# A decode-attention kernel: key loads moved four sets ahead of value loads, value products moved five sets behind scores

## The chip, the cores and the metric

The kernel runs on one core of a Trainium2 chip. The metric is device time in microseconds (us) of one execution. The core has a matrix engine (TensorE; PE in the profile, its weight loads PEld), VectorE (DVE), ScalarE (ACT), GpSimd (POOL), SyncE (SP, which here only issues transfers) and 16 DMA engines.

## The reference, cut to what matters

One decode step for a batch of 8 sequences. A layer norm of x, then attention over the last 1024 cached positions with 32 query heads and 8 key/value heads, an output projection, and a gate from a small gated feed-forward block:

```python
W = min(4096, max(256, Sk // 4))                      # 1024 of 4096 cached positions
q = (xn @ wq).reshape(B, 1, 32, 128)                  # B = 8
k, v = k_cache[:, :, Sk - W:], v_cache[:, :, Sk - W:] # 8 kv heads, 4 query heads each
p = softmax(q k^T / sqrt(128))
s = (p v).reshape(B, 1, 4096) @ wo                    # wo: 4096 x 512
g = silu((gelu(xn @ w_gate) * (xn @ w_up)) @ w_down)
out = x + s * g
```

The window of keys and that of values are 16 MiB each in bf16; with wq and wo (4 MiB each) and the feed-forward weights (5.25 MiB) 47.46 MB have to be read.

## The kernel before, in words

**Sets.** There are 64 pairs of a kv head and a sequence. Four pairs (one kv head, four sequences) make a *set*: there are NQ = 16 sets, and each has 1 MiB of keys and 1 MiB of values. A set lies in SBUF as 32 chunks of 128 x 128 (8 KB in each partition). I call the loads K0 to K15 and V0 to V15; V14 is the values of set 14. Sets 2h and 2h + 1 are kv head h, and `wo` is loaded in eight blocks of 0.5 MiB, one for each kv head, wo0 to wo7.

**Loads.** All large loads are issued by SP, in program order, at the top of the program (lines 164 to 178): four feed-forward blocks, two blocks of w_down, four of wq, then the first keys, and then in a loop over q: keys of set q + LAG, values of set q, and after every second set a block of wo. With LAG = 2 the order is K0 K1 K2 V0 K3 V1 wo0 K4 V2 ... K15 V13 wo6 V14 V15 wo7. Every load but wo takes the next of NRING = 16 buffers of `ring`, in turn; a load waits until what was in its buffer has been read.

**The main loop** (lines 523 to 546) is written out by hand in the order in which each engine's queue takes it. Step q works on the keys of set q and, LAG steps behind, on the values of set v = q - LAG, so that there are NQ + LAG steps. A step has four quarters, i = 0 to 3, one for each pair of the set:

- `transposes` (L389) of the *next* pair's eight key chunks into PSUM, evicted to `kT` by VectorE (L396) or ScalarE (L398) in turn. In quarter 3 the next pair belongs to set q + 1, so there the step first needs K(q + 1).
- in quarter 0 `sums(v)`: four matmuls (L461) for the softmax's denominators, and on VectorE their reduction and reciprocal;
- `values` (L487): eight matmuls of the pair's value chunks with the probabilities pT. Each moves VC = 4 column groups of 16 where one is needed, and VCW = 8 in the last LAG sets; only the first group of `o_ps` is used. Where the groups would run past the set, one is moved. `o_ps` has one PSUM buffer.
- in quarter 1 `max_all(q - 1)`, a transpose (L426) and three small VectorE operations (L428, L433, L436), and in quarter 2 `exponentials(q - 1)`: a matmul (L447) that adds the shift, and the exponential on ScalarE (L456), which writes pT;
- `scores` (L406) of the current pair: eight matmuls;
- in quarters 2 and 3 of every second step two heads each of `project` (L513), 16 matmuls in a step, for the kv head whose two sets are done.

After the four quarters VectorE does `normalise(v)` (L498), which reads `o_ps` and releases it, and `max_keys(q)` (L417, L421).

When the last values are done, the last four heads are projected (16 matmuls, L513), multiplied by the gate (L552), transposed (L555), added to x (L557) and stored (L558). The results of the matmuls on `idle_ps` (L256) and of the spare column groups are not read.

Of the kernel before, what the change touches and what calls it, by code (L numbers as in the profile page):

```python
# [17 lines left out]
def kernel(  # L18
# [30 lines left out]

    nc = tc.nc
    ctx.enter_context(tc.manual_schedule())

    B, Sq, D = A_x.shape
    Hkv, Sk, Dh = A_k_cache.shape[1], A_k_cache.shape[2], A_k_cache.shape[3]
# [15 lines left out]
    NCS = QG * NSC  # L72
# [6 lines left out]
    NQ = NG // QG  # L79
    QC = QG * rep  # L80
    SH = B // QG
    LAG = 2

    consts = ctx.enter_context(tc.tile_pool(name="consts", bufs=1))
    weights = ctx.enter_context(tc.tile_pool(name="weights", bufs=1))
# [1 line left out]
    ffn_sb = ctx.enter_context(tc.tile_pool(name="ffn_sb", bufs=1))  # L87
    ring = ctx.enter_context(tc.tile_pool(name="ring", bufs=NRING))
    kT_pool = ctx.enter_context(tc.tile_pool(name="kT_pool", bufs=3))
    p_pool = ctx.enter_context(tc.tile_pool(name="p_pool", bufs=4))  # L90
    small = ctx.enter_context(tc.tile_pool(name="small", bufs=2))
    ps_misc = ctx.enter_context(tc.tile_pool(name="ps_misc", bufs=1, space=PSUM))
    ps_kT = ctx.enter_context(tc.tile_pool(name="ps_kT", bufs=2, space=PSUM))
# [15 lines left out]
    NL = NCS * Dh  # L109
    q_sb, up_sb, dn_sb, k_sb, v_sb = {}, {}, {}, {}, {}  # L110

    def buffer(n):
        return ring.tile([P, NL], BF16, name="ring_sb")[:, 0:n]

    def load_set(cache, q):
        hkv, b = divmod(q * QG, B)
        t = buffer(NL)
        nc.sync.dma_start(
            out=t,
            in_=cache[b : b + QG, hkv, win0:Sk, :].rearrange(  # L120
                "g (e c) d -> e g (c d)", c=NCS
            ),
        )
        return t

    def load_k(q):
        k_sb[q] = load_set(A_k_cache, q)

    def load_v(q):
        v_sb[q] = load_set(A_v_cache, q)  # L130

    def load_q(k):
        q_sb[k] = buffer(Hq * Dh)
        nc.sync.dma_start(out=q_sb[k], in_=A_wq.rearrange("(p k) n -> p k n", k=NDC)[:, k, :])  # L134
# [20 lines left out]
    def load_wo(hkv):  # L155
        nc.sync.dma_start(
            out=wo_sb[:, hkv * rep : (hkv + 1) * rep, :],
            in_=A_wo[hkv * rep * Dh : (hkv + 1) * rep * Dh, :].rearrange(
                "(k p) d -> p k d", p=P
            ),  # L160
        )
# [6 lines left out]
        load_down(n)  # L168
    for k in range(NDC):
        load_q(k)  # L170
    for q in range(LAG):
        load_k(q)
    for q in range(NQ):
        if q + LAG < NQ:
            load_k(q + LAG)
        load_v(q)
        if q % SH == SH - 1:
            load_wo(q // SH)
# [57 lines left out]
    for i in range(2):  # L236
        t = consts.tile([MK + QG, QC], BF16, name=f"diag{i}")
# [146 lines left out]
    def transposes(g):  # L384
        q, i = divmod(g, NB)
        kT_ps = ps_kT.tile([P, W], BF16, name="kT_ps")
        for c in range(NSC):
            n = i * NSC + c
            nc.tensor.transpose(  # L389
                kT_ps[:, c * P : (c + 1) * P],  # L390
                k_sb[q][:, n * Dh : (n + 1) * Dh],
                ident,
            )
        kT[g] = kT_pool.tile([P, W], BF16, name="kT")
        if i % 2 == 0:
            nc.vector.tensor_copy(out=kT[g], in_=kT_ps)  # L396
        else:
            nc.scalar.copy(out=kT[g], in_=kT_ps)  # L398
# [80 lines left out]
    def values(g):  # L479
        q, i = divmod(g, NB)  # L480
        if i == 0:
            o_ps[q] = ps_o.tile([P, VCW, QC], FP32, name="o_ps")
        for c in range(NSC):
            n = i * NSC + c
            wide = VC if q < NQ - LAG else VCW
            wide = wide if n + wide <= NCS else 1
            nc.tensor.matmul(  # L487
                o_ps[q][:, 0:wide, :],
                v_sb[q][:, n * Dh : (n + 1) * Dh],
                pT[q][:, n : n + wide, :],  # L490
                start=(n == 0),
                stop=(n == NCS - 1),
                skip_group_check=True,
            )
# [26 lines left out]


    transposes(0)
    for q in range(NQ + LAG):
        v = q - LAG
        for i in range(NB):
            g = q * NB + i
            if g + 1 < NG:
                transposes(g + 1)
            if v >= 0:  # L530
                if i == 0:
                    sums(v)
                values(v * NB + i)
            if i == 1 and 1 <= q <= NQ:
                max_all(q - 1)
            if g < NG:
                scores(g)
            if i == 2 and 1 <= q <= NQ:
                exponentials(q - 1)
            if v >= SH and v % SH == 0 and i >= NB // 2:  # L540
                for h in range(2):
                    project((v // SH - 1) * rep + (i - NB // 2) * 2 + h)
        if v >= 0:
            normalise(v)
        if q < NQ:
            max_keys(q)
# [42 lines left out]
```

## Time and profile before

| what | value |
|---|---|
| median of 3 runs | 128.93 us (128.87 to 129.06) |
| profiled execution | 129.06 us, of which its span is 127.3 us |
| busy, share of the span | PE 81%, PEld 66%, DVE 47%, ACT 35%, POOL 1% |
| loads, share of 16 DMA engines' span | 93.4%, mean 375 GB/s over the span |
| key set load: issue to landing (median) | 19.0 us |
| value set load: issue to landing (median) | 19.0 us |
| granted TensorE clock | 1.000 |

The profile is of one execution; the span goes from the first to the last instruction, and the execution's time is 1.76 us longer than it. Times in the rows count from the span's start. "busy" of PE holds overlapping matmuls, so a matmul's mean duration is not its pitch: eight matmuls with 128 columns start some 54 ns apart while each is listed with 219 ns. An arrow in brackets names what ended the idle time before an instruction.

### The profile page before, as it was taken

How to read it: one execution, taken by the hardware profiler on the slowest of the kernel's cores; microseconds unless marked ns; L12 is line 12 of the kernel's file. 1: busy time of each engine (PE TensorE's matmuls, PEld its weight loads, DVE VectorE, ACT ScalarE, POOL GpSimd, SP SyncE). 2: the span in 40 equal slices, each digit the busy share in tenths (PEclk: the TensorE clock that was granted, in tenths of full speed). 3: DMA queues.
4: the chain of work that ended last, by engine and by line, in shares of the span. 5: the costliest groups of instructions: out<-in, count | busy, mean ns of one | idle time of the engine just before them, and what ended most of it. 6: DMA issues, size and time to landing. Idle time of an engine off the chain costs nothing.

```text
span 127.3 us, 4703 instructions
## 1 busy us (share of the span) xinstructions
PE 103.6 (81%) x2131; PEld 83.6 (66%) x2131; DVE 60.0 (47%) x189; ACT 44.5 (35%) x54; POOL 1.2 (1%) x7
## 2 busy tenths in 40 slices
PE   0999999897889987988788597769967995899880
PEld 0355646655679877877777586658956874797770
DVE  3700030101487666584765546464736674665631
ACT  4000130000646663434365434434343454354100
POOL 3000000000000000000000000000000000000000
PEclk9999999999999999999999999999999999999999
DMA  3999999999999999999999999999999999999500
GB/s 93 408 421 396 351 421 422 420 420 420 417 420 414 394 417 417 400 403 430 409 388 415 420 405 400 415 420 397 409 414 418 397 413 420 398 408 387 188 1 3
DMA packets 11860, 47.76 MB, mean 375 GB/s; under 512 B 816, under 2 KB 6720, under 8 KB 7232
## 3 DMA queue, kind: packets, MB, share of 16 engines
q1 hardware_dynamic: 11824, 47.46, 93.4%
q8 instruction: 16, 0.26, 0.8%
q10 hardware_dynamic: 16, 0.01, 0.1%
q14 instruction: 4, 0.03, 0.1%
HBM read 47.46 MB, written 0.01 MB: 373 GB/s over the span
## 4 chain that ended last, share of the span: by engine, by line
DMA 72%; PE 10%; SPq 9%; DVE 4%; ACT 1%; issue 1%; DVEq 0%
DMA ring_sb<-in_A_v_cache_dram 44%; DMA ring_sb<-in_A_k_cache_dram 28%; SPq L134 5%; PE kT_ps L389 3%; PE o_ps L487 3%; SPq L148 2%; SPq L141 2%; DVE kT L396 2%; PE sc_ps L406 2%; ACT kT L398 1%; PE sc_ps L447 1%; DVE diag L433 1%; DVE nm L428 1%; DVE diag L436 1%; PE sums_ps L461 0%
## 5 line engine op out<-in xcount | busy, mean ns | idle before, releaser
L398 ACT COPY kT<-kT_ps 128x1024 bf16<-128x1024 bf16 x32 | 32.4, 1012 | 53.9 <-PE kT_ps L389 53.9
L389 PE MATMUL kT_ps<-ident,ring_sb 128*128 128x128 bf16 x512 | 38.8, 218 | 6.0 <-DMA ring_sb<-in_A_k_cache_dram 6.0
L396 DVE COPY kT<-kT_ps 128x1024 bf16<-128x1024 bf16 x32 | 22.1, 691 | 33.5 <-PE kT_ps L389 33.5
L389 PEld LDWEIGHTS <-ring_sb 128*128 128x128 bf16 x512 | 29.2, 97 | 10.1 <-DMA ring_sb<-in_A_k_cache_dram 9.5
L487 PE MATMUL o_ps<-pT,ring_sb 128*128 128x64 bf16 (+2 forms) x512 | 25.6, 193 | 6.6 <-DMA ring_sb<-in_A_v_cache_dram 5.1
L487 PEld LDWEIGHTS <-ring_sb 128*128 128x128 bf16 x512 | 21.3, 98 | 9.4 <-DMA ring_sb<-in_A_v_cache_dram 8.4
L406 PE MATMUL sc_ps<-qT_all,kT 128*128 128x16 bf16 x512 | 22.6, 170 | 1.2 <-ACT kT L398 0.5
L406 PEld LDWEIGHTS <-kT 128*128 128x128 bf16 x512 | 18.8, 96 | 2.5 <-ACT kT L398 1.0
L256 PE MATMUL idle_ps<-ones_w 128*128 128x512 bf16 x66 | 19.6, 437 | 0.0
L417 DVE TENSOR_REDUCE mx<-sc_ps 128x16 f32<-128x512 f32 x16 | 10.9, 681 | 0.3 <-PE sc_ps L406 0.3
L456 ACT ACTIVATE pT<-sc_ps 128x512 bf16<-128x512 f32 x16 | 9.6, 598 | 3.0 <-PE sc_ps L447 3.0
L256 PEld LDWEIGHTS <-ones_w 128*128 128x128 bf16 x66 | 6.1, 106 | 6.7 <-issue 3.4
L447 PE MATMUL sc_ps<-diag,spread 68*128 68x512 bf16 x16 | 6.0, 376 | 2.3 <-DVE diag L436 0.4
L513 PEld LDWEIGHTS <-wo_sb 128*128 128x128 bf16 x128 | 4.8, 96 | 3.1 <-issue 2.3
L461 PE MATMUL sums_ps<-pT,ones_pp 128*128 128x128 bf16 x64 | 6.2, 219 | 0.1
L513 PE MATMUL sT_ps<-oT_all,wo_sb 128*128 128x8 bf16 x128 | 5.3, 166 | 0.3 <-DVE oT_all L498 0.3
L370 PEld LDWEIGHTS <-ring_sb 128*128 128x128 bf16 x128 | 3.7, 96 | 2.0 <-DMA ring_sb<-in_A_wq_dram 0.8
L469 DVE TENSOR_REDUCE recip<-sums_ps 128x16 f32<-128x128 f32 x16 | 4.5, 283 | 0.4 <-PE sums_ps L461 0.4
L498 DVE TENSOR_TENSOR oT_all<-o_ps,recip 128x16 bf16<-128x16 f32 x16 | 3.5, 220 | 2.5 <-PE o_ps L487 2.5
L428 DVE TENSOR_REDUCE nm<-mxT_ps 16x1 f32<-16x128 f32 x16 | 4.3, 270 | 0.4 <-PE mxT_ps L426 0.4
L295 PEld LDWEIGHTS <-ring_sb 128*128 128x128 bf16 x112 | 3.6, 101 | 1.3 <-issue 0.8
L461 PEld LDWEIGHTS <-ones_pp 128*128 128x128 bf16 x64 | 4.3, 98 | 0.1
(57 smaller groups left out, 45.4 us busy)
## 6 DMA issues: line engine op xcount, KB each, us to landing
ring_sb<-in_A_k_cache_dram SPq DMA_DIRECT2D x16, 1024.0 KB, 19.0
ring_sb<-in_A_v_cache_dram SPq DMA_DIRECT2D x16, 1024.0 KB, 19.0
ring_sb<-in_A_wq_dram SPq DMA_DIRECT2D x4, 1024.0 KB, 14.8
wo_sb<-in_A_wo_dram SPq DMA_DIRECT2D x8, 512.0 KB, 18.0
ring_sb<-in_B_w_gate_dram SPq DMA_DIRECT2D x2, 896.0 KB, 4.8
ring_sb<-in_B_w_up_dram SPq DMA_DIRECT2D x2, 896.0 KB, 8.2
ring_sb<-in_B_w_down_dram SPq DMA_DIRECT2D x2, 896.0 KB, 13.2
x_sb<-in_A_x_dram ACTq DMA_DIRECT2D x1, 8.0 KB
```

Source lines behind the costliest of these rows:

```text
L134: nc.sync.dma_start(out=q_sb[k], in_=A_wq.rearrange("(p k) n -> p k n", k=NDC)[:, k, :])
L256: nc.tensor.matmul(idle_ps, ones_w[:, 0:P], ones_w, start=True, stop=True)
L389: nc.tensor.transpose(kT_ps[:, c * P : (c + 1) * P], k_sb[q][:, n * Dh : (n + 1) * Dh], ident,)
L396: nc.vector.tensor_copy(out=kT[g], in_=kT_ps)
L398: nc.scalar.copy(out=kT[g], in_=kT_ps)
L406: nc.tensor.matmul(sc[q][:, i * NSC + c, :], kT[g][:, c * P : (c + 1) * P], qT_all[:, b : b + QG, hkv * rep : (hkv + 1) * rep], start=(i = ...
L417: nc.vector.tensor_reduce(out=mx, in_=sc[q].rearrange("p c n -> p n c"), axis=AX.X, op=ALU.max)
L447: nc.tensor.matmul(sc[q], spread, shift[q].unsqueeze(1).to_broadcast([MK + QG, NCS, QC]), start=False, stop=True, skip_group_check=True,)
L456: nc.scalar.activation(out=pT[q], in_=sc[q], func=ACT.Exp, scale=inv_sqrt_dh)
L461: nc.tensor.matmul(sums_ps, ones_pp, pT[q][:, c * SC : (c + 1) * SC, :], start=(c == 0), stop=(c == NCS // SC - 1),)
L487: nc.tensor.matmul(o_ps[q][:, 0:wide, :], v_sb[q][:, n * Dh : (n + 1) * Dh], pT[q][:, n : n + wide, :], start=(n == 0), stop=(n == NCS - 1 ...
L513: nc.tensor.matmul(sT_ps[0][:, d, :], wo_sb[:, h, d * P : (d + 1) * P], oT_all[:, h, :], start=(h == 0 and d == 0), stop=(h == Hq - 1), sk ...
```

## The change

LAG is split in two: LEAD = 4 says how many sets the key loads run ahead of the value loads, and LAG = LEAD + 1 = 5 how many steps the value products run behind the scores. The order of the loads becomes K0 K1 K2 K3 K4 V0 K5 V1 wo0 K6 V2 ... K15 V11 wo5 V12 V13 wo6 V14 V15 wo7, and the loop has 21 steps instead of 18. The values of the last set come in two loads, of 24 and of 8 chunks (6 KB and 2 KB in each partition), each with its own ring buffer. pT gets 7 buffers instead of 4. Chunks are handed out as lists of views, which changes no instruction. Since the line that chooses between VC and VCW compares with NQ - LAG, the eight-group form now holds for sets 11 to 15 instead of 14 and 15.

```diff
-    LAG = 2
+    LEAD = 4
+    LAG = LEAD + 1
+    VH = 3 * NCS // 4
...
-    p_pool = ctx.enter_context(tc.tile_pool(name="p_pool", bufs=4))
+    p_pool = ctx.enter_context(tc.tile_pool(name="p_pool", bufs=7))
...
-    def load_set(cache, q):
+    def load_set(cache, q, c0, c1):
+
         hkv, b = divmod(q * QG, B)
-        t = buffer(NL)
+        t = buffer((c1 - c0) * Dh)
         nc.sync.dma_start(
             out=t,
             in_=cache[b : b + QG, hkv, win0:Sk, :].rearrange(
                 "g (e c) d -> e g (c d)", c=NCS
-            ),
-        )
-        return t
+            )[:, :, c0 * Dh : c1 * Dh],
+        )
+        return [t[:, c * Dh : (c + 1) * Dh] for c in range(c1 - c0)]
 
     def load_k(q):
-        k_sb[q] = load_set(A_k_cache, q)
+        k_sb[q] = load_set(A_k_cache, q, 0, NCS)
 
     def load_v(q):
-        v_sb[q] = load_set(A_v_cache, q)
+        parts = (0, NCS) if q < NQ - 1 else (0, VH, NCS)
+        v_sb[q] = []
+        for c0, c1 in zip(parts, parts[1:]):
+            v_sb[q] += load_set(A_v_cache, q, c0, c1)
...
-    for q in range(LAG):
+    for q in range(LEAD):
         load_k(q)
     for q in range(NQ):
-        if q + LAG < NQ:
-            load_k(q + LAG)
+        if q + LEAD < NQ:
+            load_k(q + LEAD)
         load_v(q)
...
-                k_sb[q][:, n * Dh : (n + 1) * Dh],
+                k_sb[q][n],
...
-                v_sb[q][:, n * Dh : (n + 1) * Dh],
+                v_sb[q][n],
```

## The prediction

> **What bounds the kernel now.** I read the page first (slices, then the chain), then the chain of waits in order of time, then the stages around the end, then the timeline of TensorE (PE). Columns of the slices are fortieths of the span, about 3.18 us each.
>
> ```profile
> PE   0999999897889987988788597769967995899880
> PEclk9999999999999999999999999999999999999999
> DMA  3999999999999999999999999999999999999500
> ```
>
> The 16 DMA engines are busy from the second slice until about 118 us, PE never reaches its limit for long, and its granted clock is full in all slices. So until about 118 us the time is that of 47.46 MB through the queues; the change moves no byte out. What it can alter lies behind the last megabytes. The chain in order of time (start, duration, what):
>
> ```profile
> 79.21 17.96 DMA ring_sb<-in_A_v_cache_dram
> ...
> 99.72 18.05 DMA ring_sb<-in_A_v_cache_dram
> 117.76 0.05 issue
> 117.81 1.07 PE o_ps L487 x16
> ...
> 119.87 0.39 PE sc_ps L447
> ...
> 120.29 0.61 ACT pT L456
> ...
> 120.93 0.38 PE sums_ps L461 x4
> 121.32 1.57 PE o_ps L487 x32
> 122.89 0.02 issue
> 122.91 0.24 DVE oT_all L498
> 123.15 0.04 issue
> 123.19 0.56 PE sT_ps L513 x16
> ```
>
> V14 lands at 117.76. But from there the chain isn't a transfer: it is the softmax of the last key set (maximum, shift L447, exponential L456, sums L461), and only then 32 value matmuls of set 15. The stages show that V15 isn't awaited (columns: window, length, busy PE, PEld, DVE, ACT, POOL, PEclk, DMA share, GB/s):
>
> ```profile
> 118.50:119.00 0.50, 0.50 (x12) 0.49 (x10) 0.27 (x2) 0.00 (x0) 0.00 (x0) 1.00 0.60 244
> 120.50:121.00 0.50, 0.43 (x18) 0.36 (x14) 0.23 (x1) 0.38 (x1) 0.00 (x0) 1.00 0.22 70
> 121.00:121.50 0.50, 0.50 (x11) 0.50 (x11) 0.14 (x1) 0.00 (x0) 0.00 (x0) 1.00 0.02 6
> ```
>
> Everything, the last wo block behind V15 included, is in at about 121.05, and V15 about 0.5 MiB before that, near 120; its matmuls start at 121.15. The project matmuls of the last head start at 123.19; the rest of the span (4.1 us) is the output's path, which the change doesn't touch. So I count in "start of the last projection": 123.19 now.
>
> Before 117 us PE waits for both kinds of load in each step:
>
> ```profile
> 106.13 0.62 PE L389 MATMUL kT_ps<-ident,ring_sb 128*128 128x128 bf16 x8 [0.94 <-DMA ring_sb<-in_A_k_cache_dram]
> 108.63 0.41 PE L487 MATMUL o_ps<-pT,ring_sb 128*128 128x64 bf16 x8 [0.78 <-DMA ring_sb<-in_A_v_cache_dram]
> 112.72 0.61 PE L389 MATMUL kT_ps<-ident,ring_sb 128*128 128x128 bf16 x8
> 117.31 0.38 PE L461 MATMUL sums_ps<-pT,ones_pp 128*128 128x128 bf16 x4
> ```
>
> **Where the keys and values land after the change.** From V10 (79.21 + 17.96 = 97.17) to V14 (117.76) before's order moves K13, V11, wo5, K14, V12, K15, V13, wo6, V14: 7 x 1 MiB + 2 x 0.5 = 8 MiB in 20.59 us, 2.57 us per MiB. The set of loads ahead of V14 is the same after the change (all keys, V0 to V13, wo0 to wo6), so V14 still lands at 117.76. K15 now has V11, wo5, V12, V13, wo6 and V14 behind it, 5 MiB: it lands at 117.76 - 12.87 = 104.89. V11, V12 and V13 land at 107.5, 111.3 and 113.9.
>
> **Queues.** SP issues the same loads in another order, plus one. Each takes the buffer of 16 allocations earlier. The last value parts take those of V5 and K10, read by the end of step 10 (about 82.7: K11 lands 9 MiB, 23.1 us, before K15, then 0.88 us of step 10 remain); SP issues such a load about 18 us ahead of its landing, near 100. No issue waits for a buffer. That cover would have to shrink by 17 us before it cost anything. The seven probability buffers hold the six sets alive: nothing.
>
> **Steps 0 to 4 have no values.** Their evictions and scores pace them at 3.3 us (transposes of set 1 to set 2 in before), against keys every 2.57 us: PE falls 3 to 4 us behind, and wins it back, since a later step has 4.4 to 4.8 us of PE work and 5.1 or 6.4 us of loads. No cost at the end.
>
> **Steps 5 to 15.** Values come a full step early, so the two waits above become one, for the next key set, ahead of the fourth transposes: up to 6.4 - 4.6 = 1.8 us. Behind it on PE stand that quarter's values and scores; normalise and the key maximum on VectorE wait for these. The stall moves and costs nothing until the last key set. One price must be weighed: a slower PE clock through longer idling. In before PE's weight loads wait 1.53 us ahead of 106.13 and 0.95 us ahead of 108.63, in one stretch of 4 us, and PEclk stays full. I take zero. The Trainium skill ("TensorE: Matmul & The Clock Gate", HAM oscillation) puts the danger at idle gaps beyond about 3.4 us and then a halved clock; by it the sum is unchanged too, and no row here shows a gap that long in this stage.
>
> **The end, from K15 on (PE's own work).**
> - 104.94: fourth quarter of step 14, like 47.53 to 48.41: 0.88, to 105.82.
> - Step 15 has no projections in before: 112.72 to 117.31 is 4.59, less 0.26 of waiting for V13, 4.33. It now carries 16 projection matmuls (100.03 to 100.24 and 101.11 to 101.31: 0.4), partly in an eviction wait: 4.33 to 4.73, I take 4.5, to 110.32.
> - Step 16: sums, values of set 11, and the softmax of set 15 in between. In before it runs from 117.31 to the shift matmul at 119.87; without the wait for V14 the maximum's transpose can go 0.3 us sooner (mx_own is ready at 118.31, it went at 118.71). Shift at +2.25, 0.21 for it, 0.23 for the last eight values: 2.7 (3.2 if nothing is won). To 113.02.
> - A values-only set: 32 matmuls from 121.15 to a last start at 122.70 (end 122.87 less 0.17): 1.55. The eight-column-group form now holds for sets 11 to 15; it is in that row already. There is one o_ps buffer, so the next set waits for normalise: 122.70 to 123.19 is 0.49, in which the four sum matmuls fit. Even sets add 0.2 of projection (the other 0.2 lies in the 0.49).
> - Set 12: 0.49 + 1.55 + 0.2, to 115.26. Set 13: 2.04, to 117.30. PE is ready for set 14 at 117.79.
>
> V14 lands at 117.76, starts at 117.81: PE arrives level with it. Then set 14: 1.75, to 119.56; 0.49; set 15: from 120.05 to 121.60; 0.49; last projection at **122.09** instead of 123.19, a gain of 1.10. With 0.23 + 0.5 of the upper bounds PE is 0.73 late and the gain is 0.37. As level arrivals err mostly to the late side, I take **1.0**.
>
> **Last values in two parts.** Three quarters land by 119.69 at the latest, the rest by 120.33, wo7 by 121.05. They are needed at 120.05, 121.35 and 122.09. One piece at 119.95 to 120.33 would cost 0 to 0.28: the split is worth that and costs one issue. Is a split transfer slower? After V14 two loads of 1.5 MiB finish in 3.29 us, less than 1.5 x 2.57 = 3.86, so a boundary between loads cost nothing there. The Trainium skill ("DMA: Bandwidth & Descriptors", Bandwidth and the two cost components) speaks against it: at least 1 MiB a transfer, about 2.0 us fixed for each. If that 2.0 us ran in series, the small part would land near 122.3, the last projection would start near 123.0, and the gain would be 0.2; the measured boundary decides.
>
> **The sum.** The profiled execution took 129.06, its span is 127.3, 1.76 lie around it. 129.06 - 1.0 = 128.06; the median of the runs, 128.93, is 0.13 lower: 127.93, given as 127.9. This measurement can tell about 0.2%, 0.26 us, from no change.
>
> **Rivals.**
> 1. *The last transfers become the bound.* If PE is early at set 14, or V14 comes sooner, what remains is wo7 at 121.05 to 121.1: a gain of at most 2.1, 126.9. For: half the DMA engines are done by 118 (share 0.6), so V14 waits for stragglers. Against: two value sets of 1.55 and two handovers follow V14. Chance 0.15, around 127.2.
> 2. *PE's backlog eats the gain.* Upper bounds for steps 15 and 16 and a K15 that is 0.3 later: gain 0.1 to 0.4, 128.5 to 128.8. Chance 0.17.
> 3. *Slower: the values-only sets are too long.* Place: the four sets after 113.02, one output buffer each. By my rows they take 2.14 on average. From 113.02 the last projection is later than now if the mean reaches (123.19 - 113.02 - 0.49) / 4 = 2.42. The nearest row for more is before's set 14, from 117.81 to a last start at 120.52: 2.71, with the softmax inside. At 2.71 the last projection is at 124.35, plus 1.16: 130.1. Against: the softmax of set 15 is over by then. Chance 0.13; a mean of 2.55, about +0.5, 129.4, is the likelier size.
> 4. *The forecast*, 127.7 to 128.2: 0.55.
>
> Faster takes the forecast, rival 1 and a third of rival 2: 0.76. Within 0.2%: 0.11, the rest of rival 2. Slower: 0.13. The range must reach from rival 1's middle to the near side of rival 3: 127.1 to 128.9, with about 0.05 below and 0.13 above.
>
> **What would show it.** Right: waits of PE for V loads vanish before set 14, and waits for K grow to about 1.8; the key transposes end near 110 instead of 115.7; V14 still lands near 117.8 and PE waits for it little or not at all; the chain's end has no L456; values-only sets stand about 2.1 apart; last projection near 122.1. Wrong: V14 landing elsewhere by over 0.5 us, a granted clock below full, steps 17 to 20 over 2.4 us apart, or an SP issue that waits for a buffer.

## The result and the profile after

The kernel after the change takes 128.12 us (median of 4 runs, 127.86 to 128.34), the kernel before 128.98 us in the same comparison: ratio 0.9934, 95% interval 0.9911 to 0.9956. The forecast was 127.9 with a range of 127.1 to 128.9. A second comparison gave 128.09 and 129.05, ratio 0.9930 (0.9911 to 0.9948). So it is faster by 0.9 us where 1.0 was forecast. Medians here are over all runs of a kernel; the ratios leave out a run that is over 1.5% above the fastest of its kernel. The profiled execution took 127.99 us with a span of 126.3, against 129.06 and 127.3 before. Line numbers have moved by 8 in the loop's functions: transposes are L397, scores L414, values L495, project L521.

The page's slices, 3.16 us each:

```profile
PE   0999999855988988899979796894999698989981
PEclk9999999999599999999999999999679999999999
DMA  3999999999999999999999999999999999999710
```

The transfers end where they did. New are two dips of the granted clock, near 32 and near 90 us. The end of the chain of waits (start, duration, what):

```profile
99.90 18.00 DMA ring_sb<-in_A_v_cache_dram
117.90 0.05 issue
117.95 1.51 PE o_ps L495 x24
119.46 0.18 PE sT_ps L521 x8
...
120.08 0.24 PE sums_ps L469 x4
120.32 1.61 PE o_ps L495 x32
121.93 0.02 issue
121.95 0.24 DVE oT_all L506
122.19 0.04 issue
122.23 0.56 PE sT_ps L521 x16
```

V14 lands at 117.90 (117.76 before). Behind it there is no exponential any more, only two value sets with the even set's projections between them. The last projection starts at 122.23 instead of 123.19, which is the 1.0 us of the span.

TensorE's timeline from K15's landing on (start, duration, engine, line, what; in brackets the idle time and what ended it):

```profile
105.09 0.62 PE L397 MATMUL kT_ps<-ident,ring_sb 128*128 128x128 bf16 x8 [0.49 <-DMA ring_sb<-in_A_k_cache_dram]
...
110.33 0.38 PE L469 MATMUL sums_ps<-pT,ones_pp 128*128 128x128 bf16 x4
...
113.05 0.38 PE L469 MATMUL sums_ps<-pT,ones_pp 128*128 128x128 bf16 x4
...
115.49 0.38 PE L469 MATMUL sums_ps<-pT,ones_pp 128*128 128x128 bf16 x4
...
117.32 0.38 PE L469 MATMUL sums_ps<-pT,ones_pp 128*128 128x128 bf16 x4
117.95 1.51 PE L495 MATMUL o_ps<-pT,ring_sb 128*128 128x128 bf16 x24 [0.24 <-DMA ring_sb<-in_A_v_cache_dram]
```

Each row of sums opens a step. PE is idle for only 0.24 us ahead of set 14, and 0.06 to 0.07 of that isn't V14's: normalise of set 13 (L506, 117.50 to 117.73) has to release `o_ps` first. PE and V14 arrive nearly level, as forecast.

### The profile page after: what moved, and what is told of

Same layout as the page of the kernel before. It is cut to its first block, busy times and chain, and to the rows that moved or that the text cites. A ratio compares the mean times of both kernels' runs of the same rounds, so it can differ in the third digit from the quotient of the medians.

```text
span 126.3 us, 4703 instructions
## 1 busy us (share of the span) xinstructions
PE 105.6 (84%) x2126; PEld 88.0 (70%) x2131; DVE 60.7 (48%) x189; ACT 44.6 (35%) x54; POOL 1.2 (1%) x7
## 4 chain that ended last, share of the span: by engine, by line
DMA 59%; PE 20%; SPq 9%; DVE 7%; issue 2%; ACT 1%; DVEq 0%
DMA ring_sb<-in_A_k_cache_dram 44%; DMA ring_sb<-in_A_v_cache_dram 14%; PE kT_ps L397 9%; SPq L142 5%; PE o_ps L495 4%; DVE kT L404 4%; PE sc_ps L414 3%; SPq L156 3%; PE sc_ps L455 2%; SPq L149 2%; DVE diag L444 1%; DVE diag L441 1%; ACT kT L406 1%; DVE nm L436 1%; PE sT_ps L521 1%
## 5 line engine op out<-in xcount | busy, mean ns | idle before, releaser
L397 PE MATMUL kT_ps<-ident,ring_sb 128*128 128x128 bf16 x512 | 41.2, 226 | 5.4 <-DMA ring_sb<-in_A_k_cache_dram 4.3
L397 PEld LDWEIGHTS <-ring_sb 128*128 128x128 bf16 x512 | 31.4, 101 | 10.4 <-DMA ring_sb<-in_A_k_cache_dram 6.1
L495 PE MATMUL o_ps<-pT,ring_sb 128*128 128x64 bf16 (+2 forms) x512 | 26.8, 198 | 0.3 <-DMA ring_sb<-in_A_v_cache_dram 0.2
L495 PEld LDWEIGHTS <-ring_sb 128*128 128x128 bf16 x512 | 23.7, 99 | 1.4 <-issue 0.8
L414 PE MATMUL sc_ps<-qT_all,kT 128*128 128x16 bf16 x512 | 22.5, 170 | 2.0 <-ACT pT L464 0.8
L414 PEld LDWEIGHTS <-kT 128*128 128x128 bf16 x512 | 18.7, 97 | 4.1 <-ACT kT L406 1.7
L264 PE MATMUL idle_ps<-ones_w 128*128 128x512 bf16 x61 | 17.0, 411 | 0.4
L521 PEld LDWEIGHTS <-wo_sb 128*128 128x128 bf16 x128 | 4.8, 96 | 2.8 <-issue 2.1
L506 DVE TENSOR_TENSOR oT_all<-o_ps,recip 128x16 bf16<-128x16 f32 x16 | 3.6, 222 | 6.6 <-PE o_ps L495 6.6
L521 PE MATMUL sT_ps<-oT_all,wo_sb 128*128 128x8 bf16 x128 | 5.5, 166 | 1.0 <-issue 0.7
L378 PEld LDWEIGHTS <-ring_sb 128*128 128x128 bf16 x128 | 3.5, 96 | 3.9 <-DMA ring_sb<-in_A_wq_dram 3.1
L378 PE MATMUL qT_ps<-xnT_sb,ring_sb 128*128 128x8 bf16 x128 | 3.8, 166 | 2.1 <-DMA ring_sb<-in_A_wq_dram 1.7
L434 PE MATMUL mxT_ps<-ident_f,mx_own 128*16 128x128 f32 x16 | 4.5, 281 | 0.0
```

Source lines behind the costliest of these rows:

```text
L264: nc.tensor.matmul(idle_ps, ones_w[:, 0:P], ones_w, start=True, stop=True)
L378: nc.tensor.matmul(qT_ps[:, m, :], q_sb[k][:, m * Dh : (m + 1) * Dh], xnT_sb[:, k, :], start=(k == 0 and m == 0), stop=(k == NDC - 1), ski ...
L397: nc.tensor.transpose(kT_ps[:, c * P : (c + 1) * P], k_sb[q][n], ident,)
L414: nc.tensor.matmul(sc[q][:, i * NSC + c, :], kT[g][:, c * P : (c + 1) * P], qT_all[:, b : b + QG, hkv * rep : (hkv + 1) * rep], start=(i = ...
L495: nc.tensor.matmul(o_ps[q][:, 0:wide, :], v_sb[q][n], pT[q][:, n : n + wide, :], start=(n == 0), stop=(n == NCS - 1), skip_group_check=True,)
L521: nc.tensor.matmul(sT_ps[0][:, d, :], wo_sb[:, h, d * P : (d + 1) * P], oT_all[:, h, :], start=(h == 0 and d == 0), stop=(h == Hq - 1), sk ...
```

## The experiments

Theory: the gain is the last key set's softmax moved off the end; what remains is V14's landing, then two value sets on PE. Rivals: the split of the last values brings it; any lead brings it; every further set of lead brings more; the granted clock matters. Each comparison ran beside the kernel before; the change means the kernel after it.

### Without the split

```diff
-        parts = (0, NCS) if q < NQ - 1 else (0, VH, NCS)
+        parts = (0, NCS)
```

> The kernel after the change, with the values of the last set in one load again. Theory (the gain is the last key set's softmax moved off the end; the end is V14's landing and two value sets): V15 is awaited by 0 to 0.3 us at most, so 128.1 to 128.4 us, last projection at 122.2 to 122.5. Rival (the split makes the gain): back to 129.0 us, last projection near 123.2.

Measured: 128.44 us, ratio 0.9955 (0.9938 to 0.9972), just above the 128.1 to 128.4 expected and clear of the rival's 129.0. Its chain of waits:

```profile
104.56 15.56 DMA ring_sb<-in_A_v_cache_dram
120.12 0.05 issue
120.17 1.74 PE o_ps L495 x32
```

V15 in one piece lands at 120.12 and is just awaited: its sums stand at 119.69, and without the wait the values would follow at 119.95, so 0.22 us. The intervals of this kernel and of the change overlap, so a worth of about 0.2 us fits both but isn't shown by the times.

### The split alone

```diff
-    LEAD = 4
-    LAG = LEAD + 1
+    LEAD = 2
+    LAG = 2
...
-name="p_pool", bufs=7
+name="p_pool", bufs=4
```

> Only the split: LEAD 2, LAG 2, four probability buffers and the load order of before, the last values in two loads. Theory: V15 isn't awaited in before, so no change, 128.9 to 129.1 us, and the chain's end still holds the exponential L464 of set 15. Rival (the split makes the gain): 128.1 to 128.4 us.

Measured: 128.86 us, ratio 0.9984 (0.9969 to 1.0). No more than 0.3% at the outer end of the interval, and the softmax is still at the end of the chain:

```profile
120.11 0.61 ACT pT L464
...
120.76 0.38 PE sums_ps L469 x4
121.14 1.57 PE o_ps L495 x32
```

The split doesn't make the gain.

### A lead of three sets

```diff
-    LEAD = 4
+    LEAD = 3
```

> One set less: LEAD 3, LAG 4. Theory (PE's backlog behind the last key set decides): K15 has 3.5 instead of 5 MiB ahead of V14, so it lands near 108.9; with the pitches measured after the change (5 us to the end of step 15, 3.0 for step 16, 1.9 and 2.4 for odd and even value sets) PE reaches set 14 one microsecond too late, the last projection starts near 123.5, and the time is 129.0 to 129.5 us, no better than before. Rival (any lead takes the softmax off the end, V14's landing governs): 128.1 us as with LEAD 4.

Measured: 129.63 us, ratio 1.0063 (1.0033 to 1.0093): slower than before, as the backlog's sum said (a little more than its 129.0 to 129.5) and against the rival. TensorE's timeline:

```profile
108.65 0.62 PE L397 MATMUL kT_ps<-ident,ring_sb 128*128 128x128 bf16 x8 [1.01 <-DMA ring_sb<-in_A_k_cache_dram]
...
113.75 0.38 PE L469 MATMUL sums_ps<-pT,ones_pp 128*128 128x128 bf16 x4
...
119.19 1.50 PE L495 MATMUL o_ps<-pT,ring_sb 128*128 128x128 bf16 x24
...
123.46 0.54 PE L521 MATMUL sT_ps<-oT_all,wo_sb 128*128 128x8 bf16 x16 [0.32 <-DVE oT_all L506]
```

K15 lands where the order of the loads puts it (108.9 expected), set 14 starts at 119.19 with no wait for V14, and the last projection is at 123.46 (123.5 expected). The softmax is off the end here too; four value sets on PE have taken its place. This profiled execution took 129.24. The runs reach from 129.24 to 130.87 with mean clocks of 0.94 to 0.97, and the mean clock doesn't sort them: what sets the upper ones isn't shown.

### The same loads, a lag of four

```diff
-    LAG = LEAD + 1
+    LAG = LEAD
...
-            wide = VC if q < NQ - LAG else VCW
+            wide = VC if q < NQ - LEAD - 1 else VCW
```

> The loads as after the change (LEAD 4), but the values only 4 steps behind the scores, 20 steps; the eight-group form still for sets 11 to 15. Theory: the waits for keys and values are two in each step again, PE is some 1.5 us early at set 14 because one value set fewer lies behind K15, and V14's landing at 117.8 to 117.9 governs: 128.0 to 128.2 us. If the longer single waits for keys lower the granted clock, the dip near 89 us is gone here and the mean clock is nearer to 1. Rival (the fifth step itself brings the gain): 128.6 to 129.0 us.

Measured: 127.93 us (127.87 to 128.1), ratio 0.9911 (0.9891 to 0.993). PE is early, by 1.15 us where 1.5 was expected, and V14 is the floor:

```profile
118.05 1.51 PE L495 MATMUL o_ps<-pT,ring_sb 128*128 128x128 bf16 x24 [1.15 <-DMA ring_sb<-in_A_v_cache_dram]
```

So the gain needs the lead of the keys and not the fifth step of lag: the lead of three above has the same lag of four, and it lost. The dip near 90 us is absent in its profile; the longest waits for loads are 0.77 to 1.15 us. The mean clocks of its four runs, 0.959 to 0.993, overlap with those of the change (0.959 to 0.973).

### Four column groups everywhere

```diff
-            wide = VC if q < NQ - LAG else VCW
+            wide = VC
```

> The kernel after the change, with four column groups in the value matmuls of all sets instead of eight in sets 11 to 15. Theory (behind V14's landing lie two value sets of 1.55 us each): 32 matmuls of 64 columns take some 0.95 us (eight in 0.24), so set 14 ends 0.6 us sooner and the last projection waits for the last transfers instead: it starts at 121.1 to 121.5 instead of 122.23, and the time is 127.1 to 127.4 us. Rival (fewer columns lower the granted clock, and the sets take as long as now): 128.0 to 128.6 us.

Measured: 127.65 us (127.46 to 127.81), ratio 0.9888 (0.9867 to 0.991), the lowest ratio of all, though the intervals of several others overlap with it. Expected was 127.1 to 127.4; wo7 became the bound as forecast, but it landed at 121.62, so that the last projection started at 121.67 instead of 121.1 to 121.5. The chain of waits:

```profile
107.36 14.27 DMA wo_sb<-in_A_wo_dram
121.62 0.05 issue
121.67 0.57 PE sT_ps L521 x16
```

From 122 us on the granted clock was halved (0.55 in the stage from 122 to 123 us; PE had been idle for 0.98 us ahead of the last projection), and the four last transposes took 0.60 instead of 0.40 us. The mean clocks of its six runs, 0.931 to 0.957, are below those of the change (0.959 to 0.973), which fits the first half of the rival, though the cause isn't shown; the value sets did get shorter, 0.87 us for 24 matmuls instead of 1.51, against its second half.

### More output buffers

```diff
-        kT_ps = ps_kT.tile([P, W], BF16, name="kT_ps")
+        kT_ps = ps_kT.tile([P, W], BF16, name="kT_ps", tag="kT_ps")
...
-            o_ps[q] = ps_o.tile([P, VCW, QC], FP32, name="o_ps")
+            pool, tag = (ps_kT, "kT_ps") if q > NQ - LEAD - 1 else (ps_o, "o_ps")
+            o_ps[q] = pool.tile([P, VCW, QC], FP32, name="o_ps", tag=tag)
```

> The kernel after the change, with the o_ps of sets 12 to 15 in the two PSUM buffers that the key transposes no longer need. Theory (each set waits 0.45 to 0.49 us for normalise to release o_ps, of which sums fill 0.22): the handovers from 12 on go, PE is 0.5 us earlier at set 14, V14 still lands at 117.8 to 118.0, one handover of some 0.25 us goes behind it: 127.8 to 128.0 us. Rival (the handover is hidden by sums and projections): no change, 128.1 to 128.3 us.

Measured: 127.80 us, ratio 0.9901 (0.9875 to 0.9926), at the lower end of what was expected. The time fits the theory, the rows behind V14 fit the rival. From the start of the sums to that of the values set 12 takes 0.22 us here (113.15 to 113.37) and 0.46 in the change (113.05 to 113.51), but set 15 takes 0.22 (119.87 to 120.09) and 0.26 (119.94 to 120.20): behind V14 the handover shrinks by 0.04 us and not by the 0.25 expected, since sums fill most of it. What set 12 wins ends in a longer wait ahead of set 14 (0.36 us instead of 0.24). The last projection, 122.13, is 0.1 us sooner, of which 0.07 is set 14's earlier start (117.88). The rest of the 0.3 us between the two medians isn't in these positions; the intervals overlap.

### Four groups, more buffers and a lag of four

The edits of the last two, and LAG = LEAD.

> LEAD 4 and LAG 4, four column groups in all sets, two more o_ps buffers from set 12 on. Theory: only the transfers are left: wo7 lands near 121.1, the last projection starts at 121.1 to 121.4, and the time is 126.9 to 127.2 us, with V14 awaited by 1.5 us or more. Rival (the long idle time before set 14 lowers the granted clock in the last sets): sets 14 and 15 double and it is 128 us or more.

Measured: 127.76 us, ratio 0.9901 (0.9878 to 0.9923). The theory's floor was missed, and in the profiled execution by the rival's mechanism, though the time stays under the rival's 128 us. The timeline's row, and a stage of the last sets (window, length, busy PE, PEld, DVE, ACT, POOL with counts, then PEclk, DMA share, GB/s):

```profile
117.88 1.46 PE L496 MATMUL o_ps<-pT,ring_sb 128*128 128x64 bf16 x24 [2.35 <-DMA ring_sb<-in_A_v_cache_dram]
```

```profile
118.00:119.00 1.00, 1.00 (x22) 1.00 (x22) 0.00 (x0) 0.00 (x0) 0.00 (x0) 0.50 0.67 252
```

PE is so early that it waits 2.35 us for V14, and then works at half clock: 24 matmuls in 1.46 us instead of 0.87 in the kernel with four groups and a lag of five. Here the time that was won in front of V14 is paid back behind it: the last projection, 122.01, waits for PE's value sets and not for wo7.

### Filling the waits for keys

```diff
+        if i == 0 and q > LAG:
+            for _ in range(12):
+                nc.tensor.transpose(kT_ps[:, 0:P], ident, ident)
         for c in range(NSC):
```

> The kernel after the change, with 12 transposes of the identity (0.67 us) put before the first transposes of key sets 6 to 15, into the tile that these write next, so that part of the wait for each key set is filled. Nothing else is changed. Theory (the granted clock halves for 3 to 4 us after long waits for keys, and the time doesn't see it except where it falls into the last sets): the dips after 60 us go, the mean clock is 0.97 to 1.0, the runs lie closer together, the median is 127.9 to 128.2 us. Rival (the dips have another cause): the clock stays at 0.96 and the filling only costs PE up to 0.3 us, 128.1 to 128.6 us.

Measured: 132.22 us, ratio 1.0219 (1.0179 to 1.026). Both theories' sizes were wrong. The filling is 10 x 0.67 = 6.7 us of PE work; after the change PE waits for key loads only 4.3 us in all, five times, and 0.87 of that is the wait for K0. The filling didn't fill the waits, it used up all of PE's slack: the profiled execution (133.07 us, the longest of the six; span 131.3 us) doesn't show one wait for keys of 0.7 us or more behind 35 us, and its last projection is at 127.30. Its clock:

```profile
PEclk9999999975699999999999999999999999999998
```

Behind 35 us there is no dip, and the mean clocks of the six runs, 0.971 to 0.996, are in the range that the theory gave. That fits the theory on the clock, but a kernel that never waits has changed more than the clock.

### Before, with four column groups

```diff
-            wide = VC if q < NQ - LAG else VCW
+            wide = VC
```

> The kernel before, with four column groups in the value matmuls of all sets instead of eight in sets 14 and 15; loads and lag as before. Theory (two value sets and a softmax lie behind V14, all on PE): the maximum's transpose goes 0.3 us sooner, set 15 takes 0.95 instead of 1.55 us, so the last projection starts near 122.25 instead of 123.19: 128.0 to 128.2 us, as much as the change brought. Rival (the narrow form lowers the granted clock behind V14, or the softmax alone sets the pace): 128.7 us or more.

Measured: 128.29 us, ratio 0.9938 (0.9919 to 0.9958), a little behind the 128.0 to 128.2 expected: this one line in the kernel before is worth about as much as the change (0.9930 beside it). The execution that was profiled took 130.14 us with half the clock from 108 to 115 us, so it isn't read for positions. Behind 116 us its clock is full again, and there the two lengths that the theory names can be read: from the start of set 14's values to the maximum's transpose 0.61 us (119.86 to 120.47) instead of 0.90 (117.81 to 118.71), and from the sums of set 15 to the last projection 1.61 (122.69 to 124.30) instead of 2.26 (120.93 to 123.19). Together that is 0.94 us; the medians differ by 0.76.

### A lead of five sets

```diff
-    LEAD = 4
+    LEAD = 5
...
-name="p_pool", bufs=7
+name="p_pool", bufs=8
```

> One set more: LEAD 5, LAG 6, eight probability buffers; the eight-group form holds for sets 10 to 15. Theory: one value set more and one key set less behind the last key load, PE is 0.2 to 0.6 us earlier at set 14, V14's landing at 117.8 to 118.0 is the floor: 127.9 to 128.3 us, no better than LEAD 4. Rival (the gain grows with every set of lead): 127.6 us or less.

Measured: 127.95 us, ratio 0.9925 (0.9899 to 0.9951), beside 128.09 for the change again: no better, so the gain doesn't grow with the lead. The runs fall into two groups, 127.74 to 127.95 and 128.57 to 128.82. The profiled execution, 128.72, is of the upper one, and shows half clock from 104 to 107.8, just behind the wait for K15 (its timeline, and a stage in the columns of above):

```profile
102.41 0.62 PE L397 MATMUL kT_ps<-ident,ring_sb 128*128 128x128 bf16 x8 [1.66 <-DMA ring_sb<-in_A_k_cache_dram]
...
118.67 1.50 PE L495 MATMUL o_ps<-pT,ring_sb 128*128 128x128 bf16 x24
```

```profile
105.00:106.00 1.00, 1.00 (x16) 1.00 (x14) 0.20 (x1) 0.15 (x1) 0.00 (x0) 0.50 1.01 393
```

Set 14 starts at 118.67, without a wait for V14; with full clock it was expected earlier than in the change. Whether a dip is missing there in the lower group isn't shown, since no execution of that group has a profile.

### A lead of three, with four column groups

The edits LEAD = 3 and `wide = VC`.

> LEAD 3, LAG 4, with four column groups in all sets. Theory (with LEAD 3 and the wide form the loss was PE's time in the value sets behind K15): four sets that are 0.6 us shorter bring PE to set 15 before its values, the last projection starts at 121.3 to 121.8 with wo7 as the bound, and the time is 127.5 to 127.9 us. Rival (a lead of 3 is too short whatever the sets cost): 129 us or more.

Measured: 127.72 us, ratio 0.9925 (0.9892 to 0.9957). With the wide form the lead of three lost 0.6%, with the narrow form it wins 0.75%. That shows that the loss was PE's time in the value sets behind K15. Twelve runs reach from 127.34 to 129.24; the profiled one, 129.12, has a wait of 2.25 us for K15 and half clock from about 110 to 113.3. Its step 15, from the transposes behind K15's first to the sums of step 16, takes 5.40 us (110.19 to 115.59), the same stretch with the wide form 4.02 (109.73 to 113.75), at full clock: in this execution the half clock costs some 1.4 us where nothing hides it.

### The change again

> The kernel after the change, unaltered, beside the three below. Theory: 128.0 to 128.4 us, the last projection at 122.1 to 122.3 where the granted clock is full behind V14.

Measured: 128.09 us (127.93 to 128.49). V14 was awaited by 0.76 us, started at 118.05, and the last projection was at 122.33, 0.03 us later than expected.

## Why the prediction was right

**The landings held.** K15: 104.89 in the working, first transposes at 105.09. V14: 117.76 and 117.90. The order of the loads and one rate, 2.57 us per MiB, gave both; with the lead of three the first transposes of K15 start at 108.65, where the same rate gives 117.76 - 3.5 x 2.57 = 108.76.

**PE's sum from K15 on held.** Start of step 16's sums 110.32 in the working, 110.33 measured; that this is so exact is luck, since K15's transposes began 0.15 us later and step 15 took 4.36 us (105.97 to 110.33) where 4.5 was taken. Step 16 took 2.72 (2.7); sets 12 and 13 together took 4.27 (2.24 + 2.04 = 4.28). Ready at set 14: 117.79, and about 117.78 measured, when normalise of set 13 has released `o_ps`. Behind V14: 122.09 in the working, 122.23 measured; the 0.14 is V14's later landing.

**The split.** It was held to be worth 0 to 0.28 us; without it the rows show a wait of 0.22, and the times don't decide. The 2.0 us for a further load, weighed against it, would in series have brought the small part to 122.3. PE's last eight value matmuls, which read that part, were done at 121.93 and had not waited for it.

**Level arrival.** That an equal race errs to the late side wasn't seen: PE was idle ahead of set 14 for 0.24 us in one profile and 0.76 in the other. The 0.1 us that was taken off for it came true for another reason, the later landing.

**The waits for keys grew to the size forecast** (the longest 1.70 us, up to 1.8 forecast), but PE caught up with the loads much later than "wins it back" suggested: the first wait for keys behind the start is at 82 us. The prediction misread a row there. It paced the steps without values at 3.3 us, "transposes of set 1 to set 2 in before"; these are 4.10 us apart:

```profile
34.21 0.61 PE L389 MATMUL kT_ps<-ident,ring_sb 128*128 128x128 bf16 x8
...
38.31 0.61 PE L389 MATMUL kT_ps<-ident,ring_sb 128*128 128x128 bf16 x8
```

After the change the first transposes of sets 1 to 5 start 4.05 to 4.30 us apart (sets 4 and 5 at 47.71 and 51.76). Against keys every 2.57 us PE loses some 1.5 us in such a step instead of 0.7, so by the working's own sum the backlog is about twice its 3 to 4 us. Three stalls of 0.66 to 0.96 us, of which the profile names no cause for two, and a dip of the clock near 32 us added to it. It cost no time, since PE had caught up well before K15: from 82 us on it waits for keys by 0.38, 1.70, 0.86 and 0.49 us.

**The price of the clock, taken as zero, was not zero everywhere.** After the change, the longest wait in TensorE's timeline:

```profile
88.49 0.62 PE L397 MATMUL kT_ps<-ident,ring_sb 128*128 128x128 bf16 x8 [1.70 <-DMA ring_sb<-in_A_k_cache_dram]
```

and the stages behind it, in the columns of above:

```profile
90.00:91.00 1.00, 1.00 (x14) 1.00 (x12) 0.76 (x3) 0.38 (x1) 0.00 (x0) 0.50 1.04 434
93.00:94.00 1.00, 1.00 (x32) 1.00 (x31) 0.93 (x4) 0.19 (x1) 0.00 (x0) 1.00 1.05 395
```

Half clock lasts from about 89.5 to 93. It costs nothing here, because PE waits for keys again ahead of 99.88 (0.86 us). The step that failed in the prediction is the inference "PEclk stays full" from one execution: the profile of before showed no dip, but the 27 runs of before beside the first four experiments had mean clocks from 0.941 to 1.0. A granted clock below full was among the prediction's own signs of being wrong, and it came. The rule of the Trainium skill ("TensorE: Matmul & The Clock Gate", HAM oscillation), which puts the danger at idle gaps beyond some 3.4 us, would not have warned of this dip: the wait ahead of it was half as long. That the wait caused the dip is argued from how often the two come together (last section). The conclusion for the time, no cost, stood because in the profiled executions of the change no dip fell between K15 and the end. Nothing in the working secured that, so it was luck: with a lead of five, and with a lead of three and four column groups, the profiled executions have one there. Nor does the gain come from the clock: the change's mean clocks, 0.959 to 0.973, lie inside the range of those of before.

**One sign was off.** The key transposes end at 108.73 (108.12 and 0.61), not "near 110"; before ends them 1.6 us ahead of step 16, so the prediction's own 110.32 gave 108.7.

**Rivals.** Of the slower one (values-only sets too long), the four sets took (122.23 - 113.05 - 0.49) / 4 = 2.17 us on average by the prediction's formula, the wait for V14 included, where 2.42 would have decided; with one set less of lead the same backlog does decide. The transfers as the bound (rival 1) shows only in the profile with four column groups everywhere.

## What to carry to other kernels

When transfers bound the middle, count back from the last landing: everything that one in-order engine must still do behind the last load of each kind, set by set, against the landings that follow. Here reordering the loads paid until the engine arrived level with the last load; beyond that a further set brought nothing. One set less turned the gain into a loss, but only with the wide value sets: work that only fills (spare columns) belongs in the sum, since a single line on it was worth about as much as the whole reordering. Read the pace of a stage from the very rows that it will repeat; the 3.3 us above came from the wrong ones. Don't take a full clock in one profile as a property of the kernel.

## What the runs showed of the hardware that was not expected

In the 14 profiles at hand there are 16 waits of TensorE of 1.4 to 2.4 us behind 35 us; 12 of them were followed within some 2 us by half the granted clock for about 3 to 4 us, once for 7. Of 68 waits of 0.7 to 1.3 us three were. Neither length is a threshold that these runs fix, and that the wait is the cause isn't shown: the profile with the waits filled has no dip there, but no wait of 0.7 us or more for keys either, and more work on PE. What half a clock costs depends on where it falls: nothing near 90 us, 0.6 us in one value set behind V14, some 1.4 us in step 15 with a lead of three.
